# Attention with clustered masks, then a squared-ReLU feed-forward: the first batch by halves of its queries, with the mask as a matmul

## The chip, the cores and the metric

The kernel runs on one core of a Trainium2 chip. TensorE does the matrix products, VectorE and ScalarE the work on single elements, GpSimd additions in SBUF, and SyncE issues the transfers. The metric is the device time of one execution in microseconds; the time before is the median of three runs, 1306.51 us (1304.79 to 1306.89).

## The reference, cut to what matters

Each query and each key of a head is assigned to one of 16 clusters. Scores between a query and a key count only where both have the same cluster. The attention's output, eight heads of 64 side by side, is the input of a feed-forward with a squared ReLU.

```python
batch, n_heads, seq, head_dim = (4, 8, 768, 64)   # 16 clusters
q_assign = np.argmax(np.einsum('bhsd,hcd->bhsc', q_n, c_n), axis=-1)
k_assign = np.argmax(np.einsum('bhsd,hcd->bhsc', k_n, c_n), axis=-1)
mask = q_assign[:, :, :, None] == k_assign[:, :, None, :]
scores = np.where(mask, scale * np.matmul(q, k.transpose(0, 1, 3, 2)), -1000000000.0)
attn = np.exp(scores - np.max(scores, axis=-1, keepdims=True))
attn = attn / (np.sum(attn, axis=-1, keepdims=True) + 1e-09)
x = np.matmul(attn, v)                  # -> (3072, 512)
h = x @ w_in                            # w_in (512, 2048)
out = np.maximum(h, 0.0) ** 2 @ w_out   # w_out (2048, 512)
```

The weights come as 64-bit floats, which the kernel itself rounds to 32 bits.

## The kernel before, in words

**Units of work.** Two heads make a pair; there are 16 pairs, four to a batch. A pair's 768 queries are done in two halves of 384 (h), and each half in six steps (c) of 128 keys. That makes 192 steps. `scores` (L298 to L321) does one step: two matmuls, one for each head, in the upper and the lower 64 rows of the array at the same time (L302, tile sc), one exponential on ScalarE (L307, tile ex), two mask instructions on VectorE, which compare the ids of queries and keys and multiply (L309), and one addition on GpSimd into acc, the sum of the exponentials (L317, L321). `times_v` (L323) does the two products with v (L327, tile av), side by side in the columns of the array. `finish` (L335) sums acc over the keys by a matmul (L342, sm), takes the reciprocal on VectorE (L346, rb), and writes the normalised output to xT (L352), the feed-forward's input.

**Preparation of a pair** is seven items (`prep`): three times `turn` (twelve transposes, L226, copied out to qkT by ScalarE or VectorE), `logits` (L242), `route` (transposes L253, then a chain on VectorE that finds each id, L257 to L272), and twice `spread` (matmuls L279 that copy the query ids to all partitions, qid).

**Feed-forward.** `ffn` is a generator for one half of a batch: 16 times four matmuls into ph (L365), a ReLU on ScalarE (L372) and a square on VectorE (L374, gT), then three times 16 matmuls into po (L379), copied to osb and sent out. That is 64 + 48 = 112 products a half, eight halves in all. The main loop draws them one by one as filling between the steps.

**Rounding.** The weights are 32 pieces of 128 x 512; `round_weights` (L118) takes each one through eight instructions: VectorE L126, ScalarE L129, VectorE L130, L134 and L139, ScalarE L142 (and L143 on the other word), GpSimd L144 and L145. Tile w_power comes from a pool of two buffers (wtmp), w_raw from one of three (wstage).

**Order.** The main loop (from L410 on) issues a step's scores, loads one weight piece, rounds the piece loaded two steps ago, draws half of the step's filling, does one item of preparation of the next pair, then the v products of three steps ago, the finishing of five steps ago and the other half of the filling. A batch's feed-forward becomes available when its last pair is finished; its 224 products are spread over the 48 steps of the next batch. Every engine works off its instructions in order, and the framework's scheduler sets that order from the code. The PSUM tiles pt, lg, lt, pb, ph, po and sm share one pool of two buffers (ps_f).

One record of a matmul in the trace is one pass: a float32 product has two records, a bf16 product and a transpose one.

Of the kernel before, what the change touches and what calls it, by code (L numbers as in the profile page):

```python
# [17 lines left out]
P = 128  # L18
UP = 2.0 ** 40


@with_exitstack
def kernel(
# [27 lines left out]
    loads = ctx.enter_context(tc.tile_pool(name="loads", bufs=2))  # L51
    qktp = ctx.enter_context(tc.tile_pool(name="qktp", bufs=2))
    small = ctx.enter_context(tc.tile_pool(name="small", bufs=2))
    once = ctx.enter_context(tc.tile_pool(name="once", bufs=1))
# [4 lines left out]
    relup = ctx.enter_context(tc.tile_pool(name="relup", bufs=2))  # L59
# [16 lines left out]
    def load_qk(pair):  # L76
# [4 lines left out]
        for name, src in (("q_raw", q), ("k_raw", k)):  # L81
            t = loads.tile([P, NCH, 2 * D], F32, name=name)
# [7 lines left out]
    def load_v(pair):  # L90
        if pair >= NG:
            return
        b, hp = divmod(pair, HP)
        raw_v[pair] = loads.tile([P, 2, NCH, D], F32, name="v_raw")
# [57 lines left out]
    load_qk(1)  # L152
    load_v(1)
# [13 lines left out]
    good = const.tile([P, 2 * NG], F32, name="good")  # L167

# [51 lines left out]
    def turn(pair, part):  # L220
# [11 lines left out]
        if part == 2:  # L232
            raw.pop(pair)
            load_qk(pair + 2)
# [3 lines left out]
    def logits(pair):  # L238
# [7 lines left out]
        lgs[pair] = once.tile([P, TB], F32, name="lgs")  # L246
        nc.scalar.copy(out=lgs[pair], in_=lg)

    def route(pair):
        lt = bank("lt", [P, NB, P])  # L250
        src = lgs.pop(pair)
        for i in range(NB):
# [5 lines left out]
        best = once.tile([P, n, C], F32, name="best")  # L258
# [7 lines left out]
        ids[pair] = small.tile([P, NB, 4, 2], F32, name="ids")  # L266
        nc.vector.reduce_max(
            out=ids[pair].rearrange("p i g e -> p (i g e)"), in_=best, axis=AX.X
        )
        qid[pair] = [small.tile([P, NB, 2, 2], BF16, name="ids_b"),  # L270
                     small.tile([P, 2, 2, TB], BF16, name="qid")]
        nc.vector.tensor_copy(out=qid[pair][0], in_=ids[pair][:, :, 0:2])  # L272
# [12 lines left out]
    def prep(pair):  # L285
# [3 lines left out]
            lambda: spread(pair, 0), lambda: spread(pair, 1),  # L289
        ]  # L290
# [355 lines left out]
```

## Time and profile before

| | |
|---|---|
| median of 3 runs | 1306.51 us |
| the profiled execution | 1306.54 us |
| its span, first to last instruction | 1304.6 us |
| TensorE matmuls busy | 1216.2 us (93%) |
| VectorE busy | 615.6 us (47%) |
| ScalarE busy | 346.7 us (27%) |
| GpSimd busy | 391.6 us (30%) |

The shares are means over stages with different limits, so they are to be read by stage: the slices of the page first, then a table of the stages, then the timeline of single instructions.

### The profile page before, as it was taken

What the parts mean: (1) busy time and instruction counts of PE and PEld (TensorE: products, weight loads), DVE (VectorE), ACT (ScalarE), POOL (GpSimd) and SP (SyncE); (2) the same over time, 40 slices, a digit from 0 to 9 for tenths busy, and PEclk for the clock granted to TensorE, in tenths of its full rate; (3) what the DMA queues carried; (4) which work ended last, traced back from release to release, by engine and by line L of the source; (5) the groups of instructions that cost most, each with busy time, mean ns of one, the idle gap of its engine ahead of it and who ended that gap; (6) DMA issues with size and microseconds to landing.
All of it is one profiled execution on the core that took longest, in us unless ns stands there. A gap on an engine that the chain in (4) does not pass through costs nothing.

```text
span 1304.6 us, 10643 instructions
## 1 busy us (share of the span) xinstructions
PE 1216.2 (93%) x4019; PEld 496.4 (38%) x4019; DVE 615.6 (47%) x887; ACT 346.7 (27%) x555; POOL 391.6 (30%) x232
## 2 busy tenths in 40 slices
PE   7777766899999999989999999989999999999997
PEld 3222222244434433334434433334434433354553
DVE  6999999974323443454323433454323432320110
ACT  5444444322212321322212321322212311110110
POOL 3766767632212221332212221332222222200000
PEclk9775868999999999999999999999999999999999
DMA  7233323010101001000101001000000000000000
GB/s 170 81 101 96 101 95 103 12 25 0 37 17 30 15 1 53 24 21 0 37 17 33 13 1 53 29 17 0 13 17 21 1 1 17 8 1 17 8 3 24
DMA packets 62794, 42.73 MB, mean 33 GB/s; under 512 B 51472, under 2 KB 55568, under 8 KB 62736
## 3 DMA queue, kind: packets, MB, share of 16 engines
q1 hardware_dynamic: 62736, 41.98, 11.4%
q8 instruction: 33, 0.54, 0.2%
q14 instruction: 25, 0.20, 0.0%
HBM read 35.68 MB, written 6.29 MB: 32 GB/s over the span
## 4 chain that ended last, share of the span: by engine, by line
PE 76%; DVE 18%; issue 3%; POOL 2%; ACT 1%; DMA 0%; POOLq 0%; ACTq 0%
PE ph L365 27%; PE po L379 27%; PE av L327 9%; DVE ex L309 8%; PE sc L302 8%; DVE w_power L130 2%; DVE w_power L126 2%; DVE w_power L134 2%; DVE rb L346 1%; DVE w_raw L139 1%; PE pt L226 1%; PE sm L342 1%; PE lg L242 1%; PE pb L279 1%; POOL acc L321 1%
## 5 line engine op out<-in xcount | busy, mean ns | idle before, releaser
L309 DVE SCALAR_TENSOR_TENSOR ex<-qid,ids,ex 128x384 f32<-128x384 bf16 x384 | 291.4, 796 | 352.9 <-ACT ex L307 351.7
L321 POOL TENSOR_TENSOR acc<-acc,ex 128x768 f32<-128x768 f32 x128 | 242.8, 1897 | 443.9 <-DVE ex L309 429.5
L365 PE MATMUL ph<-xT,w_in 128*128 128x384 f32 x1024 | 372.3, 504 | 1.5 <-DVE qkT L229 1.5
L379 PE MATMUL po<-w_out,gT 128*128 128x512 f32 x768 | 359.8, 607 | 0.0
L327 PE MATMUL av<-ex,v_raw 128*64 128x384 f32 x768 | 233.8, 548 | 41.7 <-DVE ex L309 41.6
L307 ACT ACTIVATE ex<-sc 128x768 f32<-128x768 f32 x192 | 155.2, 810 | 373.8 <-PE sc L302 345.9
L365 PEld LDWEIGHTS ph<-xT,w_in 128*128 128x128 f32 x1024 | 183.9, 191 | 184.7 <-issue 70.1
L302 PE MATMUL sc<-qkT 64*128 64x384 f32 x768 | 205.9, 554 | 13.4 <-ACT ex L307 13.4
L379 PEld LDWEIGHTS po<-w_out,gT 128*128 128x128 f32 x768 | 136.8, 189 | 193.1 <-issue 186.1
L374 DVE TENSOR_TENSOR gT<-rl 128x384 f32<-128x384 f32 x128 | 71.8, 561 | 230.0 <-ACT rl L372 229.6
L317 POOL TENSOR_TENSOR acc<-ex 128x768 f32<-128x768 f32 x32 | 61.4, 1920 | 252.3 <-DVE ex L309 223.3
L372 ACT ACTIVATE rl<-ph 128x384 f32<-128x384 f32 x128 | 62.9, 491 | 258.4 <-PE ph L365 254.4
L302 PEld LDWEIGHTS sc<-qkT 64*128 64x128 f32 x768 | 67.6, 191 | 146.8 <-issue 111.3
L327 PEld LDWEIGHTS av<-ex,v_raw 128*64 128x64 f32 x768 | 53.6, 142 | 156.8 <-DVE ex L309 94.4
L346 DVE RECIPROCAL rb<-sm 128x384 f32<-128x384 f32 x32 | 81.7, 2553 | 36.1 <-PE sm L342 36.1
L144 POOL TENSOR_TENSOR w_raw<-w_raw 128x512 f32<-128x512 f32 x32 | 40.0, 1249 | 41.5 <-ACT w_raw L142 29.0
L386 ACT COPY osb<-po 128x512 f32<-128x512 f32 x24 | 14.1, 586 | 137.9 <-PE po L379 137.9
L283 ACT CAST qid<-pb 128x384 bf16<-128x384 f32 x64 | 29.9, 479 | 43.9 <-PE pb L279 43.9
L342 PE MATMUL sm<-acc,ups 128*64 128x384 f32 x128 | 31.9, 531 | 3.9 <-POOL acc L321 3.0
L129 ACT ACTIVATE w_power<-w_power,rebias 128x512 f32<-128x512 uint32 x32 | 22.9, 717 | 39.4 <-DVE w_power L126 39.4
L130 DVE TENSOR_SCALAR w_power<-w_power 128x512 uint32<-128x512 f32 x32 | 31.4, 981 | 0.0
L134 DVE SCALAR_TENSOR_TENSOR w_power<-w_raw,w_power 128x512 uint32<-128x512 uint32 x32 | 30.5, 953 | 0.0
(62 smaller groups left out, 398.5 us busy)
## 6 DMA issues: line engine op xcount, KB each, us to landing
w_raw<-in_moe_w_in_dram SPq DMA_DIRECT2D x16, 512.0 KB, 3.8
w_raw<-in_moe_w_out_dram SPq DMA_DIRECT2D x16, 512.0 KB, 3.5
q_raw<-in_q_dram SPq DMA_DIRECT2D x32, 192.0 KB, 3.2
k_raw<-in_k_dram SPq DMA_DIRECT2D x32, 192.0 KB, 3.3
v_raw<-in_v_dram SPq DMA_DIRECT2D x16, 384.0 KB, 3.3
out_dram<-osb SPq DMA_DIRECT2D x24, 256.0 KB, 2.0
cen<-in_centroids_dram SPq DMA_DIRECT2D x1, 32.0 KB, 1.9
```

What stands on the lines that cost most here:

```text
L130: nc.vector.tensor_scalar(out=power, in0=power_f, scalar1=float(255 << 20), scalar2=8.0, op0=ALU.min, op1=ALU.mult,)
L302: nc.tensor.matmul(sc[:, e, 0:TB], lhsT=qkT[pair][rows, NCH + c], rhs=qkT[pair][rows, NB * h : NB * (h + 1)], start=True, stop=True,)
L307: nc.scalar.activation(out=t, in_=sc[:, :, 0:TB], func=ACT.Exp, scale=SCALE)
L309: nc.vector.scalar_tensor_tensor(out=t[:, e], in0=qid[pair][1][:, h, e], scalar=ids[pair][:, c % NB, 2 + c // NB, e : e + 1], in1=t[:, e], ...
L317: nc.gpsimd.tensor_tensor(out=acc[pair, h], in0=ex[pair, h, 0], in1=t, op=ALU.add)
L321: nc.gpsimd.tensor_tensor(out=acc[pair, h], in0=acc[pair, h], in1=t, op=ALU.add)
L327: nc.tensor.matmul(av[pair, h][D * e : D * (e + 1)], lhsT=raw_v[pair][:, e, c], rhs=ex[pair, h, c][:, e], start=(c == 0), stop=(c == NCH - 1),
L346: nc.vector.reciprocal(out=rb, in_=sm)
L365: nc.tensor.matmul(ph, lhsT=w_in[:, kk, f * P : (f + 1) * P], rhs=xT[b, h][:, kk], start=(kk == 0), stop=(kk == KT - 1),)
L372: nc.scalar.activation(out=rl, in_=ph, func=ACT.Relu)
L374: nc.vector.tensor_tensor(out=gT[f], in0=rl, in1=rl, op=ALU.mult)
L379: nc.tensor.matmul(po, lhsT=gT[f][:, i * P : (i + 1) * P], rhs=w_out[:, f], start=(f == 0), stop=(f == FT - 1),)
```

## The change

**Order of units.** Steps go in twos: a unit is the scores of two steps, then the v products of the two steps that came two units earlier, then rounding, filling and up to three items of preparation. There are 96 units. The first batch is done by halves: 12 units with the first half of the queries of its four pairs, then 12 with the second half. A half's feed-forward becomes available when that half is finished, so that of the first half is spread over the 12 units of the second, and that of the second half over the 24 units of the second batch. The later batches have their 224 products spread over 24 units, as before over 48 steps.

**Mask.** For the four pairs of the first batch there are no mask instructions. `route` makes a one-hot row of 16 for each query and key (L271, tile oh), `turn_onehot` transposes them (L284), the keys' part is scaled so that equal ids give 0 and others -2^80 (L294), and `scores` adds the bf16 product of the two (L332) to sc ahead of the exponential. The later batches keep the masks on VectorE.

**Rounding** is spread: 4/3 pieces a unit in the first 12 units, two a unit from then on, in place of one a step. w_power has one buffer, w_raw two.

**Buffers.** q and k share a pool of three; qkT and ids have four; gT has 16 and takes the ReLU's output itself; osb has one.

```diff
-    loads = ctx.enter_context(tc.tile_pool(name="loads", bufs=2))
-    qktp = ctx.enter_context(tc.tile_pool(name="qktp", bufs=2))
+    loads = ctx.enter_context(tc.tile_pool(name="loads", bufs=3))
+    loads_v = ctx.enter_context(tc.tile_pool(name="loads_v", bufs=2))
+    qktp = ctx.enter_context(tc.tile_pool(name="qktp", bufs=HP))
...
-    gtp = ctx.enter_context(tc.tile_pool(name="gtp", bufs=18))
-    outp = ctx.enter_context(tc.tile_pool(name="outp", bufs=2))
-    wstage = ctx.enter_context(tc.tile_pool(name="wstage", bufs=3))
-    wtmp = ctx.enter_context(tc.tile_pool(name="wtmp", bufs=2))
+    gtp = ctx.enter_context(tc.tile_pool(name="gtp", bufs=FT))
+    outp = ctx.enter_context(tc.tile_pool(name="outp", bufs=1))
+    wstage = ctx.enter_context(tc.tile_pool(name="wstage", bufs=2))
+    wtmp = ctx.enter_context(tc.tile_pool(name="wtmp", bufs=1))
...
+        if pair < HP:
+            nc.vector.tensor_tensor(
+                out=oh.rearrange("p i g e c -> p (i g e) c")[:, :, 0:C], in0=best,
+                in1=first.unsqueeze(2).to_broadcast([P, n, C]), op=ALU.is_equal,
+            )
...
+    def turn_onehot(pair, which):
+        pt = ps_f.tile([P, NCH, P], BF16, name="po", tag="f")
+        for c in range(NCH):
+            nc.tensor.transpose(
+                out=pt[:, c],
+                in_=oh[:, c % NB, 2 * which + c // NB].rearrange("p e c -> p (e c)"),
+                identity=ident_b,
+            )
+        dst = qid[pair][1][:, which]
+        src = pt.rearrange("p c n -> p (c n)")
+        if which == 0:
+            nc.scalar.copy(out=dst, in_=src)
+        else:
+            nc.vector.tensor_scalar(
+                out=dst, in0=src, scalar1=BIG, scalar2=-BIG, op0=ALU.mult, op1=ALU.add
+            )
...
-                rhs=qkT[pair][rows, NB * h : NB * (h + 1)], start=True, stop=True,
+                rhs=qkT[pair][rows, NB * h : NB * (h + 1)], start=True, stop=pair >= HP,
+            )
+        if pair < HP:
+            for e in range(2):
+                rows = slice(D * e, D * (e + 1))
+                nc.tensor.matmul(
+                    sc[:, e, 0:TB], lhsT=qid[pair][1][rows, 1, c * P : (c + 1) * P],
+                    rhs=qid[pair][1][rows, 0, h * TB : (h + 1) * TB], start=False, stop=True,
+                )
         t = expp.tile([P, 2, TB], F32, name="ex")
         nc.scalar.activation(out=t, in_=sc[:, :, 0:TB], func=ACT.Exp, scale=SCALE)
-        for e in range(2):
+        for e in range(0 if pair < HP else 2):
...
-            rl = relup.tile([P, TB], F32, name="rl")
-            nc.scalar.activation(out=rl, in_=ph, func=ACT.Relu)
             gT.append(gtp.tile([P, TB], F32, name="gT"))
-            nc.vector.tensor_tensor(out=gT[f], in0=rl, in1=rl, op=ALU.mult)
+            nc.scalar.activation(out=gT[f], in_=ph, func=ACT.Relu)
+            nc.vector.tensor_tensor(out=gT[f], in0=gT[f], in1=gT[f], op=ALU.mult)
...
+    units = [
+        (pair, h, c)
+        for pairs, halves in [(range(HP), [0]), (range(HP), [1])]
+        + [([pair], [0, 1]) for pair in range(HP, NG)]
+        for pair in pairs for h in halves for c in range(0, NCH, 2)
+    ]
+    LAG = 2
...
+            for i in range(2):
+                scores(pair, h, c + i)
+        done = None
+        if u >= LAG:
+            pair, h, c = units[u - LAG]
+            for i in range(2):
+                times_v(pair, h, c + i)
+            if c == NCH - 2:
+                done = pair, h
+
+        rounding += 4 / 3 if u < 12 else 2
+        while rounding >= 1:
+            rounding -= 1
+            i = next(to_round, None)
+            if i is not None:
+                round_weights(i)
+                if (i := next(loaded, None)) is not None:
+                    load_weights(i)
+        share = -(-left[0] // max(1, left_units[0]))
+        left_units[0] -= 1
         fill_steps(share // 2)
+        for _ in range(3):
+            if ahead:
+                ahead.pop(0)()
+        fill_steps(share - share // 2)
+        if done:
...
+            if hp == HP - 1 and (h == 1 or b == 0):
+                for hh in [h] if b == 0 else range(2):
+                    fill.append(ffn(b, hh))
+                    left[0] += per_half
+                left_units[0] = NCH * HP // 2 if b == 0 and h == 0 else NCH * HP
```

**Where instructions stand now.** On VectorE, about a third through the rounding. A number behind a name is that of the allocated tile. Before:

```order
L130 TENSOR_SCALAR w_power_513<-w_power_513 128x512 [waits Activation_49]
L309 SCALAR_TENSOR_TENSOR ex_632<-qid_411,ids_408,ex_632 128x384 [waits PE_49]
L134 SCALAR_TENSOR_TENSOR w_power_513<-w_raw_456,w_power_513 128x512 [waits DVE_49]
L126 TENSOR_SCALAR w_power_544<-w_raw_488 128x512 [waits DMAHW6_49,Pool_49]
L139 TENSOR_SCALAR w_raw_456<-w_raw_456 128x512 [waits DVE_49]
L309 SCALAR_TENSOR_TENSOR ex_632<-qid_411,ids_408,ex_632 128x384
L229 COPY qkT_620<-pt_649 128x512 [waits PE_49]
L309 SCALAR_TENSOR_TENSOR ex_661<-qid_411,ids_408,ex_661 128x384
L130 TENSOR_SCALAR w_power_544<-w_power_544 128x512 [waits Activation_49]
```

And now:

```order
L126 TENSOR_SCALAR w_power_770<-w_raw_669 128x512 [waits DMAHW6_49,Pool_49]
L130 TENSOR_SCALAR w_power_770<-w_power_770 128x512 [waits Activation_49]
L134 SCALAR_TENSOR_TENSOR w_power_770<-w_raw_669,w_power_770 128x512 [waits DVE_49]
L139 TENSOR_SCALAR w_raw_669<-w_raw_669 128x512 [waits DVE_49]
L376 RECIPROCAL rb_829<-sm_826 128x384 [waits PE_49]
L126 TENSOR_SCALAR w_power_782<-w_raw_738 128x512 [waits DMAHW7_49,Pool_49]
L378 SCALAR_TENSOR_TENSOR ok_831,good_136<-rb_829 128x384 [waits DVE_49]
L382 SCALAR_TENSOR_TENSOR xT_518<-av_723,rb_829 128x384
L130 TENSOR_SCALAR w_power_782<-w_power_782 128x512 [waits Activation_49]
```

The masks are gone from between the rounding's instructions, and the next piece's L126 no longer stands ahead of the L139 of the piece before; its wait for GpSimd (Pool) is now one for the L145 of that piece.

On GpSimd, in the first batch. Before:

```order
L144 TENSOR_TENSOR w_raw<-w_raw 128x512
L321 TENSOR_TENSOR acc<-acc,ex 128x768
L145 TENSOR_TENSOR w_in<-w_raw,w_power 128x512
L321 TENSOR_TENSOR acc<-acc,ex 128x768
L144 TENSOR_TENSOR w_raw<-w_raw 128x512
L145 TENSOR_TENSOR w_in<-w_raw,w_power 128x512
```

And now (L347 and L351 are the additions into acc):

```order
L351 TENSOR_TENSOR acc<-acc,ex 128x768 x2
L144 TENSOR_TENSOR w_raw<-w_raw 128x512
L145 TENSOR_TENSOR w_in<-w_raw,w_power 128x512
L347 TENSOR_TENSOR acc<-ex 128x768
L144 TENSOR_TENSOR w_raw<-w_raw 128x512
L145 TENSOR_TENSOR w_in<-w_raw,w_power 128x512
L351 TENSOR_TENSOR acc<-acc,ex 128x768
L144 TENSOR_TENSOR w_raw<-w_raw 128x512
```

L144 and L145 of a piece now follow each other, and the additions stand between the pieces alone.

On TensorE, in a later batch. Before:

```order
L302 MATMUL sc<-qkT 128x384 x2
L379 MATMUL po<-w_out,gT 128x512 x3
L327 MATMUL av<-ex,v_raw 64x384 x2
L342 MATMUL sm<-acc,ups 64x384 x2
L379 MATMUL po<-w_out,gT 128x512 x3
L302 MATMUL sc<-qkT 128x384 x2
L379 MATMUL po<-w_out,gT 128x512 x3
L327 MATMUL av<-ex,v_raw 64x384 x2
```

And now (L325 scores, L357 v products, L395 ph, L227 and L243 preparation):

```order
L395 MATMUL ph<-xT,w_in 128x384 x10
L325 MATMUL sc<-qkT 128x384 x4
L357 MATMUL av<-ex,v_raw 64x384 x4
L395 MATMUL ph<-xT,w_in 128x384 x5
L227 MATMUL pt<-ident,q_raw 128x128 x4
L395 MATMUL ph<-xT,w_in 128x384 x2
L227 MATMUL pt<-ident,q_raw 128x128 x2
L227 MATMUL pt<-ident,k_raw 128x128 x2
L395 MATMUL ph<-xT,w_in 128x384
```

Scores and v products of two steps stand together, and the filling is in one or a few longer stretches.

## Rows read from the trace of the kernel before

**Rows 1.** The page's slices, 40 of the span, in tenths: TensorE and its granted clock.

```profile
PE   7777766899999999989999999989999999999997
...
PEclk9775868999999999999999999999999999999999
```

**Rows 2.** Table by stage: window, its length, busy us (instructions) by engine, clock, DMA.

```profile
12.00:240.00 228.00, 167.97 (x531) 53.56 (x529) 219.39 (x257) 110.91 (x174) 154.75 (x98) 0.77 0.33 97
...
269.00:1132.00 863.00, 852.75 (x2927) 345.91 (x2927) 341.55 (x537) 206.41 (x327) 219.17 (x118) 0.99 0.06 18
```

**Rows 3.** Timeline of TensorE: start us, us, instruction, records; its first feed-forward and the tail.

```profile
268.84 4.54 PE L365 MATMUL ph<-xT,w_in 128*128 128x384 f32 x8 [1.51 <-DVE qkT L229]
...
1132.38 41.70 PE L365 MATMUL ph<-xT,w_in 128*128 128x384 f32 x128
1173.92 41.36 PE L379 MATMUL po<-w_out,gT 128*128 128x512 f32 x96
...
1297.69 0.19 PE L448 MATMUL every<-ups,fine 128*1 128x1 f32 x2
```

**Rows 4.** Table by stage of line L307 alone, the exponentials with one table load.

```profile
0.00:268.84 268.84, 44.52 (x55) 0.80 0.34 95
268.84:1304.60 1035.76, 111.97 (x138) 0.99 0.06 17
```

**Rows 5.** Groups of VectorE's instructions up to 268.84 us: count, busy us, mean ns, idle before.

```profile
L309 DVE SCALAR_TENSOR_TENSOR ex<-qid,ids,ex 128x384 f32<-128x384 bf16 x105 | 119.0, 1158 | 1.0 <-ACT qid L283 1.0
...
L346 DVE RECIPROCAL rb<-sm 128x384 f32<-128x384 f32 x7 | 17.8, 2545 | 0.0
...
L263 DVE TENSOR_TENSOR best<-best,order 128x384 f32<-128x384 f32 x5 | 2.7, 548 | 0.0
```

**Rows 6.** Timeline from 35 to 46 us: one rounding, and an addition ahead of it.

```profile
35.02 1.80 POOL L321 TENSOR_TENSOR acc<-acc,ex 128x768 f32<-128x768 f32 x1
...
35.10 2.01 DVE L126 TENSOR_SCALAR w_power<-w_raw 128x512 uint32<-128x512 uint32 x1 [1.19 <-POOL w_in L145]
...
37.14 0.72 ACT L129 ACTIVATE w_power<-w_power,rebias 128x512 f32<-128x512 uint32 x1 [5.66 <-DVE w_power L126]
...
39.91 0.41 DVE L130 TENSOR_SCALAR w_power<-w_power 128x512 uint32<-128x512 f32 x1
...
40.72 0.67 DVE L134 SCALAR_TENSOR_TENSOR w_power<-w_raw,w_power 128x512 uint32<-128x512 uint32 x1
...
41.78 0.41 DVE L139 TENSOR_SCALAR w_raw<-w_raw 128x512 uint32<-128x512 uint32 x1
...
42.23 0.68 ACT L142 ACTIVATE w_raw<-w_raw 128x512 f32<-128x512 uint32 x1 [1.90 <-DVE w_raw L139]
...
42.98 1.45 POOL L144 TENSOR_TENSOR w_raw<-w_raw 128x512 f32<-128x512 f32 x1 [3.41 <-ACT w_raw L142]
...
44.51 1.48 POOL L145 TENSOR_TENSOR w_in<-w_raw,w_power 128x512 f32<-128x512 f32 x1
```

**Rows 7.** Timeline, three more of rounding: another L144, a later round's L126 and its L145.

```profile
205.04 1.05 POOL L144 TENSOR_TENSOR w_raw<-w_raw 128x512 f32<-128x512 f32 x1
...
220.31 0.41 DVE L126 TENSOR_SCALAR w_power<-w_raw 128x512 uint32<-128x512 uint32 x1
...
232.82 1.61 POOL L145 TENSOR_TENSOR w_out<-w_raw,w_power 128x512 f32<-128x512 f32 x1
```

**Rows 8.** Timeline of TensorE in the second batch.

```profile
329.87 0.87 PE L327 MATMUL av<-ex,v_raw 128*64 128x384 f32 x4
330.67 2.20 PE L365 MATMUL ph<-xT,w_in 128*128 128x384 f32 x6
332.80 0.92 PE L302 MATMUL sc<-qkT 64*128 64x384 f32 x4
333.65 2.20 PE L365 MATMUL ph<-xT,w_in 128*128 128x384 f32 x6
```

**Rows 9.** Timeline of TensorE where packs of one kind follow each other.

```profile
206.77 1.56 PE L302 MATMUL sc<-qkT 64*128 64x384 f32 x8
...
1125.31 2.16 PE L327 MATMUL av<-ex,v_raw 128*64 128x384 f32 x12
```

More of the change, by code (lines that the diff above doesn't have):

```diff
@@ L19 @@
 UP = 2.0 ** 40
+BIG = 2.0 ** 80
 @with_exitstack
@@ L90, in load_v @@
     def load_v(pair):
-        if pair >= NG:
-            return
         b, hp = divmod(pair, HP)
-        raw_v[pair] = loads.tile([P, 2, NCH, D], F32, name="v_raw")
+        raw_v[pair] = loads_v.tile([P, 2, NCH, D], F32, name="v_raw")
         nc.sync.dma_start(
@@ L233, in turn @@
             raw.pop(pair)
-            load_qk(pair + 2)
+            load_qk(pair + 1)
     lgs = {}
@@ L245, in logits @@
             )
-        lgs[pair] = once.tile([P, TB], F32, name="lgs")
+        lgs[pair] = rbp.tile([P, TB], F32, name="lgs", tag="rb")
         nc.scalar.copy(out=lgs[pair], in_=lg)
@@ L257, in route @@
         nc.vector.reduce_max(out=mx, in_=lt, axis=AX.X)
-        best = once.tile([P, n, C], F32, name="best")
+        best = once.tile([P, n, C], BF16, name="best")
         nc.vector.tensor_tensor(
@@ L288, in prep @@
             lambda: logits(pair), lambda: route(pair),
-            lambda: spread(pair, 0), lambda: spread(pair, 1),
-        ]
+        ] + [lambda i=i: (turn_onehot if pair < HP else spread)(pair, i) for i in range(2)]
     ex = {}
@@ L388, in ffn @@
             yield
-    LAG = 3
-    DONE = 5
-    steps = [(pair, h, c) for pair in range(NG) for h in range(2) for c in range(NCH)]
+    units = [
[5 more added lines that the diff above has]
+    LAG = 2
     per_half = FT * KT + NB * FT
@@ L404, in fill_steps, with next_pair @@
                 left[0] -= 1
+    def next_pair(u):
+        pair, h, c = units[u]
+        if c == 0 and pair + 1 < NG and h == 0 and (pair + 1) not in qkT:
+            if pair + 1 < HP or pair >= HP:
+                return pair + 1
+        if c == 0 and h == 1 and pair == HP - 1:
+            return pair + 1
+        return None
+    to_round = iter(range(len(weights)))
+    loaded = iter(range(len(weights)))
     centroids_norm()
@@ L409 @@
     ahead = []
-    for n in range(len(steps) + DONE):
-        if n < len(steps):
-            pair, h, c = steps[n]
-            if h == 0 and c == 0 and pair + 1 < NG:
-                ahead = prep(pair + 1)
-            scores(pair, h, c)
-            if n < len(weights):
-                load_weights(n)
-            if 0 <= n - 2 < len(weights):
-                round_weights(n - 2)
-        share = -(-left[0] // max(1, 2 * NCH * HP - n % (2 * NCH * HP) - 2))
-        fill_steps(share // 2)
-        if ahead and n % 12 >= 2:
-            ahead.pop(0)()
-        if 0 <= n - LAG < len(steps):
-            times_v(*steps[n - LAG])
-        if 0 <= n - DONE < len(steps):
-            pair, h, c = steps[n - DONE]
-            if c == NCH - 1:
-                finish(pair, h)
-                if h == 1:
-                    b, hp = divmod(pair, HP)
-                    for d in (qkT, ids, qid, raw_v):
-                        d.pop(pair)
-                    load_v(pair + 2)
-                    if hp == HP - 1:
-                        fill.extend(ffn(b, hh) for hh in range(2))
-                        left[0] += 2 * per_half
-        fill_steps(share - share // 2)
+    left_units = [0]
@@ new lines @@
+    rounding = 0.0
+    for _ in range(2):
+        load_weights(next(loaded))
+    for u in range(len(units) + LAG):
+        if u < len(units):
+            pair, h, c = units[u]
+            if (p := next_pair(u)) is not None:
+                ahead.extend(prep(p))
+            if c == 0 and pair not in raw_v:
+                load_v(pair)
+            for i in range(2):
[17 more added lines that the diff above has]
+        left_units[0] -= 1
+        fill_steps(share // 2)
+        for _ in range(3):
+            if ahead:
+                ahead.pop(0)()
+        fill_steps(share - share // 2)
+        if done:
+            pair, h = done
+            finish(pair, h)
+            b, hp = divmod(pair, HP)
+            if h == 1:
+                for d in (qkT, ids, qid):
+                    d.pop(pair)
+            if h == 1 or b == 0:
+                raw_v.pop(pair)
+            if hp == HP - 1 and (h == 1 or b == 0):
[3 more added lines that the diff above has]
+                left_units[0] = NCH * HP // 2 if b == 0 and h == 0 else NCH * HP
```

24 lines of the change are left out of this document (12 added, 12 removed).

## The prediction, before the changed kernel ran

> **What bounds the kernel now.** I read the page's slices and the table by stage first. TensorE is busy nine tenths or more of nearly every slice from the ninth on, but only six to eight tenths before, and there its granted clock falls to half in many slices [rows 1]. Between 12 and 240 us VectorE is busy 219 of 228 us and TensorE 168, at a mean clock of 0.77; between 269 and 1132 us TensorE is busy 853 of 863 us at 0.99 [rows 2]. So there are two kernels in one: the first batch (all four of its head pairs, with the 32 weight pieces rounded beside them) goes at the pace of VectorE and GpSimd, and everything after the first feed-forward matmul, at 268.84 us, goes at TensorE's pace [rows 3].
>
> The second part can be split. After the attention has ended, two halves of the feed-forward run alone from 1132.38 to 1297.69 us: 165.3 us, 82.7 each, 41.5 us for 64 products into ph and as much for 48 into po [rows 3]. Eight halves are 661 us. The whole second part lasts 1028.9 us; the other 368 us belong to the attention steps still to do. By the count of exponentials, 54 of the 193 less one table load (192) lay before 268.84 us [rows 4], which leaves 138, or 69 pairs of steps at 5.33 us a pair, all stalls in it.
>
> Why is the first part slow? A mask instruction on VectorE takes 1158 ns there on the mean [rows 5]. The timeline shows the reason with a rounding instruction: GpSimd starts an addition at 35.02 us, VectorE starts L126 at 35.10, and it ends when the addition has ended, after 2.01 us instead of the 0.41 us of another L126 [rows 6, 7]. VectorE and GpSimd take turns here.
>
> **The change part by part.** *Masks of the first batch to TensorE.* 96 mask instructions leave VectorE, 111 us at the mean of rows 5. 96 short bf16 matmuls join TensorE. No row shows one; they lie between nothing and one float32 pair of scores (0.85 us [rows 8]) per step, so 0 to 41 us, and I take 10, since the operand is streamed once and not in two passes. TensorE had 60 us free in that stage [rows 2] and gets more free time, so they cost the sum nothing. Building the one-hot operands costs four pairs two VectorE instructions each, about 0.55 us as L263 is [rows 5], beside twelve transposes; spreading of ids (L279, L283) leaves in exchange.
>
> *Rounding with fewer buffers.* This is where I expect the new bound. w_power has one buffer instead of two, w_raw two instead of three. The order shows L126 of each round waiting for GpSimd, and behind the last L139: a round now starts only after L145 of the round before. Behind that L126, in order, stand the next pair's routing, rb and xT on VectorE, and through L129 and L142 on ScalarE the exponentials. So the 32 rounds are one chain, and its length sets when the first 22 of 96 units (two steps each) are through: 44 exponentials stand ahead of the last L142 on ScalarE. One round with nothing in its way: L126 0.41, L129 0.72, L130 0.41, L134 0.67, L139 0.41, L142 0.68, L144 1.05 to 1.45, L145 1.48 [rows 6, 7]; eight handovers of 0.03 to 0.08 us as between the rows shown; 6.2 us in all. 32 of them: 198 us. Between L145 of one round and L144 of the next, GpSimd's order has additions in 23 places, 36 in all. The first of a place starts at once and holds L126 off, as at 35.02, and costs its 1.80 us; a further one overlaps L129 and costs 1.1. Together 56 us. VectorE's preparation between L126 and L139, what of rb (2545 ns [rows 5]) L144 and L145 do not hide, and waits for ScalarE behind an exponential: I take 15 us, 0.5 us a round, between 0 and 2 us. With 10 us ahead of the first round the chain ends at 279 us, 8.4 us a round. Before, two rounds were under way at once.
>
> *First half of the queries first.* The order has the first ph ahead of unit 15, so at the chain's end TensorE has done all 64 ph of the first half and 15 of its 48 po; the sixteenth po needs the last piece of w_out. That is where the gain is: of 661 us of feed-forward 41.5 + 12.9 = 54 us are done inside the first batch, and 22 units of attention. Remaining: 608 us of feed-forward and 74 units.
>
> *Steps in twos.* Before, two steps cost TensorE two packs of scores at 0.85 us (332.80 to 333.65), two of v products at 0.80 and four stretches of feed-forward, each with 0.18 us beyond its matmuls (six ph records take 2.13 us from 330.67 to 332.80, six at the pace of the tail 1.95) [rows 3, 8]: 4.02 us. In twos: a second pack behind its like adds 0.64 us (eight records of sc take 1.56 us, four take 0.92; twelve of av 2.16, four 0.87) [rows 8, 9]. So 0.85 + 0.64 + 0.80 + 0.64 and one stretch, 3.11. I take 0.85 of the 0.91 saved, because preparation cuts a stretch in half the units: 5.33 - 0.85 = 4.48 us a unit, 74 units 331 us. The Trainium skill (TensorE: Matmul & The Clock Gate, Part 3, The mechanism) says that a weight load overlaps a running matmul only where the row group differs; by it the second pack would reload the same rows and pay its full 0.85 and 0.80, and the sum would be 27 us higher. The rows show 0.64, so I go by them.
>
> *Edits with no cost in the sum.* gT written by ScalarE and squared in place: the same two instructions. 16 gT buffers and not 18: the first is read out sixteen po before the next half wants it. One osb: its copy waits for a 2 us transfer, under the 13.8 us of the next sixteen po [rows 3]. On SP, q, k and v loads now stand behind w_raw loads that wait for L145; they are needed three units, four rounds, later, and if that cover went, TensorE's transposes and behind them scores would wait a round, 8 us.
>
> The sum: 279 + 608 + 331 + 6.9 (1297.7 to the end of the span of 1304.6) = 1225 us of span. The profiled execution took 1306.54 us, 1.9 more than its span, and equals the median of 1306.51: 1227 us.
>
> **The rivals.** *Additions fit into the gaps.* If the exponentials come late enough for L126 to take its turn first, additions run under ScalarE's L129 and L142 and cost nothing: the chain ends at 223 us, the time is 1171. For it: VectorE is free of masks. Against: at 35.02 the addition won. *The chain stays as long as a round takes now (slower).* Rounds in the trace take 10.9 us from L126 to the end of L145 (35.10 to 45.99) and 14.1 (220.31 to 234.43) [rows 6, 7]. These have masks and a second round in between. If the waits come from GpSimd's additions and ScalarE's queue instead, one buffer makes this latency the period: at 12.3 us the chain ends at 404 us and the time is 1352. It decides from 10.9 us a round, where the span is again 1304. *TensorE doesn't get faster units.* Three preparation items per unit share two PSUM buffers with the feed-forward, so each waits for the copy of the one before; if these stalls, or half clock in the gaps, eat the 0.85 us, 74 units cost 63 us more: 1290. Against: the order puts feed-forward between them. That the early feed-forward doesn't happen at all is excluded by the order.
>
> **How the numbers follow.** The forecast has 0.63, additions in the gaps 0.17, no faster units 0.12, the long chain 0.08. The forecast's own bounds are 0.6 us a round either way (19 us) and 0.15 us a unit (11 us). The range, 1178 to 1285, takes these in and the near ends of the first and third rivals, and leaves out the long chain. About 0.2% is what a measurement can tell from no change; faster by more: 0.63 + 0.17 + 0.09 = 0.89; within it 0.03 (the edge between the last two rivals); slower 0.08.
>
> **What would show it.** Right: L126 with idle time ended by L145 in nearly every round, L145 to L145 some 8.4 us, the last at about 280 us; first ph near 170 us; TensorE not much over six tenths busy until then and full afterwards; units of 4.5 us beyond feed-forward in the last two batches; the last attention step some 80 us earlier than before, the tail unchanged at 165 us. Wrong: L145 intervals under 7 or over 10 us; TensorE idle behind pt or lt in the later batches; masked scores that wait for the one-hot copy so that ScalarE, not the rounding, is waited for.

## The result

The changed kernel takes 1233.31 us (1232.32 to 1233.67, four runs) where the kernel before takes 1306.70 beside it: 0.9439 of the time, 95% interval 0.9423 to 0.9455. The forecast was 1227. The profiled execution has a span of 1231.4 us and took 1233.24.

The page's slices of the kernel after, TensorE and its granted clock, answer to [rows 1]:

```profile
PE   6677776689999999999999999999999999999997
...
PEclk7877798879999999999999999999999999999999
```

The first nine slices look as they did: six to eight tenths busy, at a clock between half and full. From the tenth on TensorE is full, and the stretch of full slices is shorter than before. The table by stage of the kernel after (window, its length, busy us and instructions of each engine, clock, DMA share, GB/s) answers to [rows 2]:

```profile
12.00:275.50 263.50, 188.88 (x724) 82.00 (x725) 143.01 (x196) 111.04 (x173) 142.81 (x100) 0.79 0.28 83
275.50:1061.40 785.90, 779.77 (x2934) 347.98 (x2933) 412.94 (x543) 204.23 (x330) 236.26 (x125) 1.00 0.09 23
1061.40:1223.50 162.10, 162.10 (x441) 83.17 (x440) 18.39 (x36) 18.27 (x37) 0.00 (x0) 1.00 0.02 8
```

The columns are TensorE, its weight loads, VectorE, ScalarE, GpSimd. In the first batch VectorE has gone from 96% busy to 54%, yet TensorE is still busy only 72% of the time, at about the old clock. So the masks left VectorE, and something else holds TensorE there. Groups of waits of the kernel after between 12 and 275.5 us (waiter, what it waited for: us, times, longest):

```profile
ACT w_power L129 <- DVE w_power L126: 82.0, 29, 4.8
...
DVE w_power L126 <- POOL w_out L145: 39.9, 15, 5.5
DVE w_power L126 <- POOL w_in L145: 34.7, 14, 4.2
...
PE ph L395 <- ACT gT L402: 26.3, 6, 8.7
...
PE lt L254 <- ACT lgs L248: 11.7, 3, 6.7
PE po L284 <- DVE oh L271: 11.5, 3, 6.6
```

29 of the 32 rounds begin with a wait for the round before. ScalarE stands idle 82 us in front of L129, and most of TensorE's waits are for ScalarE, which does its copies and gT in one order with the rounds. Two rounds in the timeline of the kernel after:

```profile
256.59 0.43 DVE L126 TENSOR_SCALAR w_power<-w_raw 128x512 uint32<-128x512 uint32 x1 [5.48 <-POOL w_out L145]
257.06 0.72 ACT L129 ACTIVATE w_power<-w_power,rebias 128x512 f32<-128x512 uint32 x1 [0.60 <-DVE w_power L126]
...
260.21 1.04 POOL L144 TENSOR_TENSOR w_raw<-w_raw 128x512 f32<-128x512 f32 x1 [3.65 <-ACT w_raw L142]
261.33 1.29 POOL L145 TENSOR_TENSOR w_out<-w_raw,w_power 128x512 f32<-128x512 f32 x1
262.66 0.43 DVE L126 TENSOR_SCALAR w_power<-w_raw 128x512 uint32<-128x512 uint32 x1 [2.77 <-POOL w_out L145]
...
274.25 1.29 POOL L145 TENSOR_TENSOR w_out<-w_raw,w_power 128x512 f32<-128x512 f32 x1
```

From 256.59 to 262.66 is a round with nothing in its way, 6.07 us. The first L126 starts at 12.5 us and the last L145 ends at 275.5: 263 us, 8.2 us a round. From the end of one L145 to the next, a round with no addition ahead of it takes 6.1 to 7.5 us, with one 6.9 to 10.7, with two or three 9.1 to 13.1.

TensorE's timeline after, the start of the feed-forward, the masked scores, a unit of the second batch, and the tail:

```profile
148.06 2.90 PE L395 MATMUL ph<-xT,w_in 128*128 128x384 f32 x6
...
258.35 2.74 PE L408 MATMUL po<-w_out,gT 128*128 128x512 f32 x6
261.02 0.92 PE L325 MATMUL sc<-qkT 64*128 64x384 f32 x4
261.76 0.33 PE L332 MATMUL sc<-ohT 64*128 64x384 bf16 x2
261.93 0.81 PE L325 MATMUL sc<-qkT 64*128 64x384 f32 x4
262.57 0.33 PE L332 MATMUL sc<-ohT 64*128 64x384 bf16 x2
262.83 1.51 PE L357 MATMUL av<-ex,v_raw 128*64 128x384 f32 x8
...
494.40 1.56 PE L325 MATMUL sc<-qkT 64*128 64x384 f32 x8
495.90 1.51 PE L357 MATMUL av<-ex,v_raw 128*64 128x384 f32 x8
497.34 2.84 PE L408 MATMUL po<-w_out,gT 128*128 128x512 f32 x6
...
1058.17 41.70 PE L395 MATMUL ph<-xT,w_in 128*128 128x384 f32 x128
...
1223.48 0.19 PE L515 MATMUL every<-ups,fine 128*1 128x1 f32 x2
```

The tail lasts 165.3 us as before, and the last attention step is 74 us earlier. At 275.5 us TensorE has done all 64 ph and 9 po of the first half, and the scores of 22 units and the v products of 20. 955.9 us follow: 612 of feed-forward, 7.8 behind the tail, so 336 for 75 units (the mean of 74 and 76), 4.48 us each. A count that needs no such mean agrees: from the first scores of the third batch to those of the fourth, 24 units, 264.6 us pass with 128 ph and 86 po in them, 4.47 us a unit beyond these (in the kernel before 293.0 us with 128 and 96, 5.30).

One measure makes the experiments readable. In nearly every run built on the kernel after, TensorE is full from 310 us on, with 11 to 13 us idle behind that point (19 in e6), so the span follows how much TensorE has got done by then: its idle time up to 310 us, and the clock it was granted while busy. Stage table of the kernel after, cut there (columns as above):

```profile
0.00:310.00 310.00, 227.41 (x864) 99.29 (x864) 153.10 (x227) 120.14 (x188) 152.29 (x113) 0.82 0.29 84
310.00:1320.00 1010.00, 908.35 (x3253) 416.91 (x3251) 425.49 (x568) 216.05 (x356) 229.00 (x120) 1.00 0.07 18
```

82.6 us idle, 908 us of TensorE left. The kernel before, in the same cut, has 71.4 us idle and 978 left, with units that cost more.

### The profile page after: what moved, and what is told of

It reads as the page before. It is cut to its first block, busy times and chain, and to the rows that moved or that the text cites. A ratio compares the mean times of both kernels' runs of the same rounds, so it can differ in the third digit from the quotient of the medians.

```text
span 1231.4 us, 10628 instructions
## 1 busy us (share of the span) xinstructions
PE 1135.8 (92%) x4115; PEld 516.2 (42%) x4115; DVE 578.6 (47%) x795; ACT 336.2 (27%) x543; POOL 381.3 (31%) x233
## 4 chain that ended last, share of the span: by engine, by line
PE 77%; POOL 8%; issue 8%; DVE 4%; ACT 2%; DMA 0%; SPq 0%; POOLq 0%; ACTq 0%
PE po L408 27%; PE ph L395 24%; PE sc L325 10%; PE av L357 9%; POOL acc L351 3%; POOL w_raw L144 2%; PE sm L372 2%; PE pt L227 2%; POOL w_out L145 1%; POOL w_in L145 1%; DVE w_power L126 1%; PE pb L303 1%; PE lg L243 1%; ACT ex L337 1%; DVE ids L269 0%
## 5 line engine op out<-in xcount | busy, mean ns | idle before, releaser
L395 PE MATMUL ph<-xT,w_in 128*128 128x384 f32 x1024 | 361.6, 502 | 27.4 <-ACT gT L402 26.3
L351 POOL TENSOR_TENSOR acc<-acc,ex 128x768 f32<-128x768 f32 x128 | 245.9, 1921 | 398.1 <-DVE ex L339 322.6
L408 PE MATMUL po<-w_out,gT 128*128 128x512 f32 x768 | 349.9, 602 | 0.0
L339 DVE SCALAR_TENSOR_TENSOR ex<-qid,ids,ex 128x384 f32<-128x384 bf16 x288 | 229.1, 847 | 157.9 <-ACT ex L337 157.7
L395 PEld LDWEIGHTS ph<-xT,w_in 128*128 128x128 f32 x1024 | 189.9, 193 | 186.9 <-issue 32.3
L325 PE MATMUL sc<-qkT 64*128 64x384 f32 x768 | 195.0, 546 | 12.2 <-ACT ex L337 12.2
L403 DVE TENSOR_TENSOR gT<-gT 128x384 f32<-128x384 f32 x128 | 91.8, 721 | 177.7 <-ACT gT L402 177.4
L357 PE MATMUL av<-ex,v_raw 128*64 128x384 f32 x768 | 161.9, 521 | 0.0
L402 ACT ACTIVATE gT<-ph 128x384 f32<-128x384 f32 x128 | 62.5, 488 | 250.8 <-PE ph L395 250.8
L325 PEld LDWEIGHTS sc<-qkT 64*128 64x128 f32 x768 | 77.0, 197 | 105.1 <-issue 64.2
L376 DVE RECIPROCAL rb<-sm 128x384 f32<-128x384 f32 x32 | 81.7, 2554 | 80.6 <-PE sm L372 80.6
L347 POOL TENSOR_TENSOR acc<-ex 128x768 f32<-128x768 f32 x32 | 58.4, 1826 | 174.7 <-DVE ex L339 153.3
L357 PEld LDWEIGHTS av<-ex,v_raw 128*64 128x64 f32 x768 | 50.8, 141 | 93.3 <-issue 91.5
L126 DVE TENSOR_SCALAR w_power<-w_raw 128x512 uint32<-128x512 uint32 x32 | 32.6, 1020 | 78.0 <-POOL w_out L145 39.9
L144 POOL TENSOR_TENSOR w_raw<-w_raw 128x512 f32<-128x512 f32 x32 | 33.3, 1040 | 79.9 <-ACT w_raw L142 79.9
L129 ACT ACTIVATE w_power<-w_power,rebias 128x512 f32<-128x512 uint32 x32 | 23.1, 722 | 82.0 <-DVE w_power L126 82.0
L307 ACT CAST qid<-pb 128x384 bf16<-128x384 f32 x48 | 21.9, 480 | 40.2 <-PE pb L303 40.0
L142 ACT ACTIVATE w_raw<-w_raw 128x512 f32<-128x512 uint32 x32 | 21.4, 668 | 41.7 <-DVE w_raw L139 41.7
```

Of the source, the lines that this page charges most:

```text
L144: nc.gpsimd.tensor_tensor(out=hi_f, in0=hi_f, in1=lo_f, op=ALU.add)
L325: nc.tensor.matmul(sc[:, e, 0:TB], lhsT=qkT[pair][rows, NCH + c], rhs=qkT[pair][rows, NB * h : NB * (h + 1)], start=True, stop=pair >= HP,)
L339: nc.vector.scalar_tensor_tensor(out=t[:, e], in0=qid[pair][1][:, h, e], scalar=ids[pair][:, c % NB, 2 + c // NB, e : e + 1], in1=t[:, e], ...
L347: nc.gpsimd.tensor_tensor(out=acc[pair, h], in0=ex[pair, h, 0], in1=t, op=ALU.add)
L351: nc.gpsimd.tensor_tensor(out=acc[pair, h], in0=acc[pair, h], in1=t, op=ALU.add)
L357: nc.tensor.matmul(av[pair, h][D * e : D * (e + 1)], lhsT=raw_v[pair][:, e, c], rhs=ex[pair, h, c][:, e], start=(c == 0), stop=(c == NCH - 1),
```

## The experiments

Theory: the twos give their 0.85 us a unit, and the first batch's pace is the chain of rounds with its additions. Rivals: the chain is only a symptom; the masks or the halves make the gain; packs behind their like save less. All the kernels below are compared with the kernel after, 1233.3 us. The kernel before took 1307.0 to 1309.0 us beside them and 1306.7 beside the kernel after, so differences of some 2 us say nothing.

### The twos undone (e5)

The later three batches go back to one step at a time, feed-forward in four stretches; the first batch stays as changed.

```diff
+        ones = second is not None and second[0] >= HP
...
+        if ones:
+            for i in range(2):
+                if first:
+                    scores(*first[:2], first[2] + i)
+                fill_steps(parts[2 * i])
...
+                times_v(*second[:2], second[2] + i)
...
+                fill_steps(parts[2 * i + 1])
```

> Twos undone in the second to fourth batch: a unit is scores, filling, v products, filling, twice over, as before; the first batch, its order and its rounding are as in the changed kernel. Theory (each change between packed and full matmuls costs TensorE, 0.85 us a unit in all): 72 units, 61 us more, 1294. Rival by the Trainium skill (TensorE: Matmul & The Clock Gate, Part 3, The mechanism; a weight load overlaps only where the row group differs, so a second pack saves nothing and only the stretches of filling count): a half of it, 1268. Rival (other engines set the pace there): within 5 us of 1233.

Measured: 1294.48 us (1293.80 to 1294.89), 61.2 us slower. 72 units lie in those batches: 0.85 us a unit, as the forecast has it. Its timeline of TensorE, second batch, shows the price of single packs:

```profile
522.30 0.92 PE L325 MATMUL sc<-qkT 64*128 64x384 f32 x4
523.15 1.13 PE L408 MATMUL po<-w_out,gT 128*128 128x512 f32 x2
524.20 0.87 PE L357 MATMUL av<-ex,v_raw 128*64 128x384 f32 x4
```

From the start of the scores to what follows them is 0.85 us here, 1.50 for two packs in the kernel after (494.40 to 495.90). The last L145 ends at 276.1 us and unit 24 begins at 309.8, as in the kernel after, so nothing in the first batch explains the difference. This run also says what all the rest of the change is worth, with the twos in the first batch: 1294.5 against 1307.1 for the kernel before, 12.6 us.

### The masks back on VectorE (e6)

```diff
-        if pair < HP:
+        if pair < 0:
...
-        for e in range(0 if pair < HP else 2):
+        for e in range(2):
...
```

> The mask of the first batch back on VectorE, with the ids spread as in the later batches; halves, twos and the rounding's buffers stay. Theory (masks stand in the chain of rounds on VectorE): 3 masks a round, 0.6 us each, 58 us more, 1290. Rival (VectorE waits for L145 for a good part of the stage and the masks fit in there, and the framework's order now has only 26 rounds ahead of unit 24 instead of 32): unit 24 starts near 272 us instead of 310, time 1195 to 1233.

Measured: 1239.11 us (1238.51 to 1240.22), 5.8 us slower. Both views missed the time, and both had a part right. With the masks back the chain is longer: its last L145 ends at 309.7 us, 34 later. And the order does have only 26 rounds ahead of unit 24 on ScalarE instead of 32: that unit begins at 266.9 us instead of 309.7. Its stage table and its group of mask instructions up to 310 us:

```profile
0.00:310.00 310.00, 228.26 (x791) 94.42 (x792) 220.50 (x321) 125.84 (x202) 158.62 (x113) 0.86 0.29 84
```

```profile
L339 DVE SCALAR_TENSOR_TENSOR ex<-qid,ids,ex 128x384 f32<-128x384 bf16 x102 | 88.2, 894 | 4.7 <-ACT ex L337 3.3 <-ACT qid L307 1.2
```

VectorE takes on 67 us more work (220 of 310 us). TensorE's idle time is 81.7 us, as in the kernel after, at a higher clock, and the same 908 us are left. The 5.8 us lie behind 310: TensorE is idle 18.7 us there instead of 13.0, and one wait makes that up. VectorE is busy with masks of the second batch before it copies k for TensorE's next transposes:

```profile
316.43 9.97 DVE L339 SCALAR_TENSOR_TENSOR ex<-qid,ids,ex 128x384 f32<-128x384 bf16 x7
...
326.32 0.68 DVE L230 COPY qkT<-pt 128x512 f32<-128x512 f32 x1
327.06 1.11 PE L227 MATMUL pt<-ident,k_raw 128*128 128x128 f32 x4 [6.05 <-DVE qkT L230]
```

A mask takes 894 ns, not the 1158 of [rows 5]. So the masks moved the chain by 34 us and the time by 6. What they would cost with the order held no run shows, nor how far VectorE's fill bounded the kernel before.

### The first batch without halves (e7)

```diff
-        for pairs, halves in [(range(HP), [0]), (range(HP), [1])]
-        + [([pair], [0, 1]) for pair in range(HP, NG)]
+        for pairs, halves in [([pair], [0, 1]) for pair in range(NG)]
...
```

> The first batch pair by pair, both halves of a pair in turn, its feed-forward after all of it, as in the later batches; mask on TensorE, twos and rounding as in the changed kernel. Recorded view (the halves give TensorE feed-forward to do while it waits for the rounds, 32 rounds come first in either case): the 67 us of feed-forward that the changed kernel has done by unit 24 are lost but for some waits, time near 1279. Rival (what counts is how many rounds stand ahead of a unit in the order: 25 ahead of unit 24 here, 32 there): unit 24 at 12 + 25 x 8.2 = 217 us, and 921 + 67 us after it, 1206: faster without halves.

Measured: 1249.56 us (1248.55 to 1250.69), 16.2 us slower. The direction is that of the recorded view, the size a third of it. Its stage table up to 310 us:

```profile
0.00:310.00 310.00, 213.08 (x895) 89.92 (x895) 193.78 (x259) 128.72 (x200) 175.09 (x123) 0.81 0.29 81
```

96.9 us idle, 14.3 more than with halves. The first ph starts at 263 us, not at 148, but the attention does not stand still meanwhile: unit 24 of the 96 begins at 235 us instead of 310, with 25 rounds ahead of it on ScalarE instead of 32, though the last L145 ends at 300.0 us, 24 later. What the halves move into the first batch as feed-forward they take out of it as attention.

### A second buffer for w_power (e1)

Odd rounds use the buffer of osb, which the first batch hardly needs.

```diff
-        power = wtmp.tile([P, NW], U32, name="w_power")
+        pool = outp if i % 2 else wtmp
+        power = pool.tile([P, NW], U32, name="w_power", tag="osb" if i % 2 else "w_power")
...
```

> One part of the change undone: w_power has two buffers again (every second round takes the buffer of osb, which is idle until the rounding is over); w_raw keeps two. Theory (one chain of rounds sets the first 275 us of the changed kernel, 8.2 us a round): VectorE's part of the next round now runs beside GpSimd's part of this one, the period falls towards 6.6 us, the period of the kernel before, the last L145 ends near 225 us instead of 275 and the time falls by some 50 us, from 1233 to about 1185. Rival (the pace is set by GpSimd's additions and ScalarE's queue, the single buffer is beside the point): last L145 within 8 us of 275, time within 8 us of 1233.

Measured: 1211.34 us (1208.73 to 1211.65), ratio to before 0.9252 (0.9228 to 0.9276): 22 us faster. It lies halfway between the two views. The last L145 ends at 238.8 us, 37 earlier. Its waits of VectorE up to 240 us (L127 is L126 there) and its stage table:

```profile
DVE w_power L127 <- DMA w_raw<-in_moe_w_in_dram: 23.0, 7, 5.0
DVE w_power L131 <- ACT w_power L130: 21.1, 23, 2.6
DVE w_power L127 <- DMA w_raw<-in_moe_w_out_dram: 16.3, 13, 2.7
```

```profile
0.00:310.00 310.00, 241.92 (x943) 104.72 (x944) 175.67 (x239) 125.63 (x195) 164.50 (x116) 0.84 0.31 88
```

The wait for the round before is gone, and the next one is late instead: the load into w_raw, which still has two buffers. Idle time falls from 82.6 to 68.1 us, and 887 us are left instead of 908. The order moved as well: 27 rounds stand ahead of unit 18 on ScalarE instead of 24. A third buffer for w_raw was not run.

### A link more in the chain (e2)

```diff
+        nc.scalar.mul(out=hi_f, in_=hi_f, mul=1.0)
```

> The changed kernel with one more link in each round: after L142 ScalarE multiplies the same word by 1.0 again, 0.67 us and a handover of 0.07. Theory (the rounds are one chain that nothing hides): 32 x 0.74 = 24 us more, 1257. Rival (the rounds have slack, another engine's order sets the pace): no more than 5 us.

Measured: 1236.73 us (1235.05 to 1237.56), 3.4 us slower, which is not clear of noise: its ratio to before is 0.9448 (0.9425 to 0.9471), that of the kernel after 0.9439. Yet the last L145 ends at 309.8 us, 34 later. A chain that is 34 us longer costs almost nothing here, so the theory in its simple form fell. Two things gave way. The order in which the framework lays out the work shifted with the edit: on ScalarE 16 rounds stand ahead of unit 16, 20 ahead of unit 18 and 28 ahead of unit 22, where the kernel after has 19, 24 and 32. Unit 24 begins at 311.8 us instead of 309.7. And the clock rose, as its stage table shows:

```profile
0.00:310.00 310.00, 216.74 (x847) 94.05 (x848) 158.49 (x223) 135.37 (x216) 153.77 (x113) 0.85 0.29 83
310.00:1250.00 940.00, 913.04 (x3269) 418.36 (x3268) 428.97 (x572) 218.30 (x359) 229.10 (x120) 1.00 0.07 20
```

10.7 us more idle, but only 4.7 us more left at 310. Which of the two gave way more no run separates.

### The first batch's additions taken out (e3)

```diff
-        elif c > 1:
+        elif c > 1 and pair >= HP:
```

> The changed kernel without GpSimd's additions of steps 2 to 5 in the first batch; its sums hold the first two steps alone (part of the computation is left out). Of 36 additions between the rounds 8 are left. Theory (an addition between two rounds holds L126 off and costs 1.8 us, a second one in the same gap 1.1): 41 us less in the rounds, last L145 near 234 us, time near 1192. Rival (the additions fit into the gaps of the chain): last L145 still near 275, time near 1233.

Measured: 1195.61 us (1194.74 to 1198.08), ratio to before 0.9136 (0.9114 to 0.9158): 37.7 us faster. The order has the rounds where the kernel after has them, within one (10 instead of 9 ahead of unit 8), so this run is the clean test that the one before was not. The last L145 ends at 241.1 us, 34.4 earlier. With the order held, the time follows the chain about one to one.

```profile
0.00:310.00 310.00, 251.71 (x1003) 110.38 (x1004) 140.74 (x251) 131.48 (x205) 101.69 (x86) 0.91 0.31 89
310.00:1320.00 1010.00, 873.77 (x3116) 402.17 (x3112) 408.65 (x545) 205.70 (x339) 220.26 (x116) 1.00 0.06 17
```

58.3 us idle, a clock of 0.91, 874 us left.

### The first batch's additions on VectorE (e8)

```diff
-            nc.gpsimd.tensor_tensor(
+            (nc.vector if pair < HP else nc.gpsimd).tensor_tensor(
...
```

> The additions of the first batch on VectorE instead of GpSimd; nothing else changed. Theory (between two rounds an addition on GpSimd holds L126 off for 1.8 us; on VectorE it takes some 0.85 us, by the 0.56 us of a 384-wide operation): 36 x 0.9 = 32 us less in the rounds, time near 1201. Rival (VectorE, in order, now stands in front of its own L126 and the gain is gone): 1225 to 1240.

Measured: 1199.95 us (1199.14 to 1200.59), ratio to before 0.9176 (0.9156 to 0.9196): 33.4 us faster than the kernel after, with the whole computation. The groups that changed, first of the kernel after up to 275.5 us (mean ns behind the comma):

```profile
L126 DVE TENSOR_SCALAR w_power<-w_raw 128x512 uint32<-128x512 uint32 x32 | 32.6, 1020 | 78.0 <-POOL w_out L145 39.9 <-POOL w_in L145 34.7 <-DMA w_raw<-in_moe_w_in_dram 3.4
```

```profile
L351 POOL TENSOR_TENSOR acc<-acc,ex 128x768 f32<-128x768 f32 x28 | 53.2, 1900 | 31.0 <-ACT ex L337 30.6
```

then of this kernel up to 310 us:

```profile
L351 DVE TENSOR_TENSOR acc<-acc,ex 128x768 f32<-128x768 f32 x32 | 31.2, 976 | 6.0 <-ACT ex L337 5.7
...
L126 DVE TENSOR_SCALAR w_power<-w_raw 128x512 uint32<-128x512 uint32 x32 | 13.6, 426 | 60.6 <-POOL w_out L145 34.0 <-POOL w_in L145 23.1 <-DMA w_raw<-in_moe_w_in_dram 3.4
```

An addition takes 0.98 us on VectorE and 1.90 on GpSimd. L126 takes 426 ns where it took 1020, 19 us less over the 32 rounds, because no addition holds it off. The chain ends at 252.2 us, 23.3 earlier.

```profile
0.00:310.00 310.00, 249.50 (x991) 108.78 (x993) 168.85 (x289) 129.38 (x203) 89.61 (x77) 0.86 0.30 89
```

60.5 us idle, and 876 us left. VectorE had the room for this (169 of 310 us busy); whether it would have it with the masks as well was not run. The time gained 10 us more than the chain; the order moved a little too (22 rounds ahead of unit 18 and 31 ahead of unit 22, where the kernel after has 24 and 32), and how much of the 10 us that is stays open.

### Both: additions on VectorE, two buffers for w_power (e9)

The edits of e8 and e1 together.

> The first batch's additions run on VectorE and w_power has two buffers, both of the edits that gave 33 and 22 us singly. Theory: what is lost in the first batch is TensorE's idle time and its slow clock while units wait behind rounding rounds in ScalarE's order; with the additions gone from GpSimd a round still takes 7.5 us because its first instruction waits for the round before (57 us of waits of L126 for L145), and with a second buffer that wait goes, so the rounds end near 215 us instead of 252 and the time falls to about 1180 us (20 us below the additions on VectorE alone). Rival: with the additions gone the rounds no longer bound the first batch, and TensorE's other waits (the router, the rectified values, the copies of q and k) do; then the second buffer gives under 5 us and the time is 1195 to 1203 us. A time over 1205 us would say that rounds that overlap each other crowd ScalarE and VectorE.

Measured: 1189.44 us (1187.64 to 1190.77), ratio to before 0.9096 (0.9081 to 0.9111), the fastest of all. The second buffer is worth 10.5 us more here, between the two views. The last L145 ends at 229.5 us, not at 215: the waits for the round before are gone, and what L126 waits for now is the load into w_raw (20.3 us in 16 waits); a round takes 6.8 us.

```profile
0.00:310.00 310.00, 255.98 (x1035) 111.97 (x1036) 203.05 (x299) 132.16 (x208) 97.21 (x80) 0.90 0.31 89
```

54.0 us idle, at a clock of 0.90, and 865 us left (908 in the kernel after).

### One buffer in the kernel before (e4)

The fewer buffers, and nothing else of the change.

```diff
-    wstage = ctx.enter_context(tc.tile_pool(name="wstage", bufs=3))
-    wtmp = ctx.enter_context(tc.tile_pool(name="wtmp", bufs=2))
+    wstage = ctx.enter_context(tc.tile_pool(name="wstage", bufs=2))
+    wtmp = ctx.enter_context(tc.tile_pool(name="wtmp", bufs=1))
```

> The kernel before with the changed kernel's buffers for the rounding: one w_power, two w_raw; masks stay on VectorE. Theory (with one buffer the length of a round becomes the period, and masks stand in it): a round of 9.5 to 12.3 us instead of 6.6, over 32 rounds 95 to 180 us more than 1307. Rival (the masks find room where VectorE waits for L145): under 20 us more.

Measured: 1290.19 us (1290.05 to 1290.33), ratio 0.9861 (0.9832 to 0.9891): 19 us faster than the kernel before beside it (1308.98), where a loss was expected by the one view and little change by the other. The rounds take 6.1 to 14.0 us and the last ends at 340 us instead of 240, and still the last xT of the first batch is written by 223.4 us instead of 275.3. The order explains where the time could come from: 15 rounds stand ahead of unit 24 on ScalarE, where the kernel before has all 32.

```profile
0.00:310.00 310.00, 233.00 (x869) 86.50 (x870) 249.52 (x347) 129.09 (x209) 175.20 (x116) 0.86 0.29 79
```

TensorE is idle longer (77.0 us against 71.4) at a clock of 0.86 instead of 0.82, and has 955 us left instead of 978. VectorE and GpSimd also met less often: a mask took 1031 ns on the mean up to 222.9 us, where [rows 5] has 1158. How much of the 19 us is the order and how much is this stays open; no run separates them.

## Why the prediction was right, and where its steps were off

**The units in twos: right.** 4.48 us a unit were forecast and 4.48 measured, and undoing the twos costs 0.85 us a unit (e5). The Trainium skill (TensorE: Matmul & The Clock Gate, Part 3, The mechanism) says that weight loads overlap a running matmul only where the row group differs. What the forecast, and the rival in e5, drew from it, that a second pack pays in full, is contradicted here: a second pack adds 0.65 us.

**The chain: right in length, off in its terms.** 279 us forecast, 275.5 measured, 8.4 and 8.2 us a round. The first round began at 12.5 us, not 10. A bare round takes 6.07 us (6.2 forecast), 194 in all. Of the other 69 us, taking out the 28 additions that lay in the chain gave 34 (e3), 1.2 each; the 36 forecast at 56 us come to about 44, an estimate from that. The 15 us of queueing were then about 25. The forecast let the first addition of each of the 23 places hold L126 off; it did so in 12 (L126 of 2.01 us), and in the other 11 L126 went first. The two errors cancel, so that the length came out so near is in part luck. The mean hides a wide spread, too: of 31 intervals from L145 to L145, 12 are under 7 us and 5 over 10, the bounds that the forecast named.

**What the chain decides: right only with the order held.** "Its length sets when the first 22 of 96 units are through" stands for the kernel as it is, and for e3 about one to one. It is not a law of this kernel: 34 us more of chain cost 3.4 in e2 and 5.8 in e6, 24 more cost 16 in e7, where the halves are gone too, 37 less gave 22 (e1), 23 less gave 33 (e8). How many rounds the order puts ahead of a unit, times the round's period, does better: it puts unit 22 of e2 at 273 us (28 rounds of 9.25 from 13.6; measured 272) and unit 24 of e7 at 237 (measured 235). But it puts unit 24 of e6 at 254, and that began at 267, so it is not the whole either.

**"That is where the gain is": wrong.** The forecast put that on the 54 us of feed-forward done inside the first batch. By its own sum 74 units at 0.85 us, 63 us, are most of the gain, and e5 measured 61 for the 72 of the later batches. The halves are worth 16 (e7). The balance with e7 at 275.5 us shows why: the kernel after has 64 ph and 9 po done, 49 us, and e7 13 ph, 8 us; but it has 6 units of attention less, at 4.48 us each 27 us: 41 - 27 = 14.

**9 po and not 15; first ph at 148 and not 170.** The sixteenth po was thought to be the limit. TensorE waited earlier: for ScalarE, which copies its transposes and makes gT behind the rounds in its queue (26.3 us in 6 waits of ph for gT, one of 8.7). The 6 us by which the forecast fell short are these po (612 us of feed-forward left, not 608; the forecast's own terms give 661 - 54 = 607), one unit more (75, not 74: the v products lag two units behind the scores, 4.5 us) and 0.9 us behind the tail, less 3.5 us of chain.

**The masks: right that TensorE takes them for little, wrong in what leaving VectorE would bring.** They cost 0.17 to 0.26 us a step at the full clock (261.76 to 261.93, 262.57 to 262.83), 8 to 12 us for 48 steps, as taken, and 0.29 to 0.46 in the steps at half clock (0.50 from 65.90 to 66.90 us). TensorE also waited 11.5 us for the one-hot rows, about as long as for the ids in e6 (10.7). But the 111 us that left VectorE are worth 6, with the order as it falls in e6. Nearly half of what masks took before looks like turns with GpSimd: the median mask up to 268.84 us takes 0.61 us, so that the 105 of [rows 5] would need 64 of their 119 us, an estimate from that median.

**The rivals.** Additions in the gaps: half true, with L126 held off in 12 of the 23 places. Its price of 1171 us was too low all the same: even without 32 of the first batch's 40 additions the time is 1195.6 (e3). The long chain: rounds of 10.5 to 13.1 us came, five of 31, four of them among five rounds from 78 to 132 us, but they did not last. And a single buffer is not harmful by itself in the kernel before (e4), though a second one gives 22 us in the kernel after (e1). No faster units: fell with e5.

## What to carry to other kernels

Price what a change saves on the engine that is full for most of the span first: 0.85 us in 72 places outweighed the whole rebuilding of the first stage. In a stage where no engine is full, ask what the full engine waits for and through which queue, then remove the operation that holds that queue's owner off (here the additions on GpSimd, 33 us), not the one that fills the busiest row. Before a buffer count or one instruction more is judged by its wait, look at how it moves the order of the rest: in e2, e4 and e6 the chain of rounds grew by 34 to 100 us and the time rose by 6 at most, or fell, while the order shifted. That the order is the reason is a reading of these runs; none held everything else.

## What the runs showed of the hardware

L126 on VectorE, which works on SBUF, waits out a GpSimd addition that started before it: 2.01 us instead of 0.43, in 12 of the kernel after's 32 rounds. In its timeline:

```profile
90.62 1.80 POOL L351 TENSOR_TENSOR acc<-acc,ex 128x768 f32<-128x768 f32 x1
90.70 2.01 DVE L126 TENSOR_SCALAR w_power<-w_raw 128x512 uint32<-128x512 uint32 x1 [4.20 <-POOL w_in L145]
```

It is not so for all of VectorE's instructions: the reciprocals, which read PSUM, took 2545 ns on the mean in [rows 5] and 2555 in e8 without additions on GpSimd.

The time did not follow TensorE's idle time in the first 310 us alone, because the mean granted clock moved too, to either side: 82.6 us idle at 0.82 in the kernel after, 58.3 at 0.91 in e3, but 93.3 at 0.85 in e2. The clock is not a function of the idle time alone; which pattern of work earned 0.85 with more idle time in e2 no run here tells.
